# Moving weights, gate parts and X to other places in SBUF: a spectral layer with a gated FFN in float32r

## The chip, the cores and the metric

One core of one Trainium2 chip runs the whole program. The metric is the device time of one execution in microseconds; lower is better.

## The reference

For each of 8 sequences of 3008 rows and 256 channels, the reference takes a real FFT along the sequence, multiplies by a complex 256x256 weight, shrinks real and imaginary parts towards zero by 0.01, transforms back, and then runs a feed-forward layer over all 24064 rows:

```python
X = np.fft.rfft(x, axis=1)
Yr = Xr @ w_r - Xi @ w_i + b_r
Yi = Xr @ w_i + Xi @ w_r + b_i
Y* = sign(Y*) * max(abs(Y*) - 0.01, 0)
y = np.fft.irfft(Y, n=3008, axis=1)
h = y @ w_in                    # 256 -> 2048
g = h * clip(h + 3, 0, 6) / 6
out = g @ w_out                 # 2048 -> 256
```

The weights w_in and w_out come as float64, the output is float32.

## The kernel before

Each float32 operand is split into a high and a low part in float32r, and a product is three matmuls: low weight by high data, and high weight by high and by low data (`product`, line 137 is its matmul). The FFT is done as two small transforms (47 and 64 points) by matmuls, one sequence at a time: `stage1` (xs against f47), `middle` (bt against f64; then X against w_r, w_m and w_i, which stream while a block of X is the stationary operand; then z against g64) and `segment` (qt against f47, which writes `raw`, a tile of 512 output columns).

The FFN runs over 47 chunks c of 512 rows and, within each, over 8 bands f of 256 hidden columns: 376 units. In `prepare` the chunk's activations become seven blocks yb of 128x256, which are combined with seven 128x128 blocks of w_in per band (a Strassen-like scheme: `block`, in `phase_1`, `phase_2`, `phase_b` to `phase_e`): 21 matmuls of 256 columns. `gate` turns a unit's hidden values h into g, high and low part, in the tile `gs`: ScalarE's relu (line 1091), VectorE's multiply (line 1093), ScalarE's high part (line 1096), VectorE's low part (line 1097). `down` multiplies by w_out into two accumulators po0 and po1: 12 matmuls of 512 columns.

The order is written out by hand: the last loop goes unit by unit, with phases of unit i, of i - 1, the gate of i - 1 and i - 2, and four groups of `down` of i - 3, and between them `fill` puts one step of the FFT of the next sequence, by slots laid out in advance. So the engines' queues have a fixed order, and PE's is a mix of groups of three matmuls of each kind. The weights are made ready in the first hundred microseconds by the class `Band` (`upper`, `lower`, `sums_hi`, `sums_lo`), between the steps of the first sequence's FFT.

Tiles are laid out in SBUF in the order in which they are made, each at a multiple of 32 bytes in every partition: the constants first (weights among them), then the shared buffers by tag. The line `space([P, 24], F32, "gap")` makes a tile that nothing uses; what is made for the first time after it (X, z, the small buffers) lies 96 bytes further on. Each w_in band has 7 blocks of 512 bytes in a high and in a low tile, each w_out band 4 blocks of 512 bytes in each, so that all of them lie at the same place modulo 256.

Of the kernel before, what the change touches and what calls it, by code (L numbers as in the profile page):

```python
# [9 lines left out]
F32 = mybir.dt.float32  # L10
F32R = mybir.dt.float32r
# [3 lines left out]
ALU = mybir.AluOpType  # L15
# [6 lines left out]
B, S, D, FF = 8, 3008, 256, 2048  # L22
# [3 lines left out]
P = 128  # L26
# [4 lines left out]
NFT = FF // P  # L31

T = 512
# [68 lines left out]
def spectral_ffn(ctx: ExitStack, tc: tile.TileContext, x, w_r, w_i, bias, w_in, w_out, f47, f64, g64, g64u, sgn, out):  # L102
    nc = tc.nc
    const = ctx.enter_context(tc.tile_pool(name="const", bufs=1))
# [9 lines left out]
    def space(shape, dt, name, tag=None):  # L114
        tag = tag or name
        return sb.tile(shape, dt, name=name, tag=tag, bufs=depth.get(tag, 1))
# [11 lines left out]
    def split(hi, lo, src, on=None):  # L128

        nc.scalar.copy(out=hi, in_=src)  # L130
        (on or nc.vector).tensor_tensor(out=lo, in0=src, in1=hi.bitcast(F32), op=ALU.subtract)  # L131

    def product(ps, terms, start=True, stop=True, more=False, later=False):

        todo = [p for (ah, al), (bh, bl) in terms for p in (((al, bh), (ah, bh), (ah, bl)) if later else ((al, bh), (ah, bl), (ah, bh)))]
        for n, (a, b) in enumerate(todo):
            nc.tensor.matmul(  # L137
                out=ps,
                lhsT=a,
                rhs=b,  # L140
                start=start and n == 0,
                stop=stop and n == len(todo) - 1,
                skip_group_check=more,
            )
# [13 lines left out]
    nf = NFT // 2  # L158
# [8 lines left out]

    win_s = [const.tile([P, nf, 7, P], F32R, name="w_in_" + t) for t in ("hi", "lo")]  # L170
    wout_s = [const.tile([P, NFT * D], F32R, name="w_out_" + t) for t in ("hi", "lo")]
    under = const.tile([P, 1], F32, name="under")
    nc.vector.memset(under, -LAM)

# [27 lines left out]
    class Band:  # L202
# [56 lines left out]
        def upper(self):  # L259
            if self.into:  # L260
                nc.scalar.copy(out=win_s[0][:, self.f, :3], in_=self.value[:, 1:])
            else:
                nc.scalar.copy(out=wout_s[0][:, self.f * 512 : (self.f + 1) * 512], in_=self.top)

        def lower(self):
            f = self.f
            if not self.into:
                on = nc.gpsimd if f < nf - 2 else nc.vector
                on.tensor_tensor(
                    out=wout_s[1][:, f * 512 : (f + 1) * 512], in0=self.rf, in1=self.base, op=ALU.mult  # L270
                )

        def sums_hi(self):
# [18 lines left out]
    def band():  # L292

        n = len(bands)
        if n < len(todo_bands):
            bands.append(Band(*todo_bands[n], LATE.get(n) or SETS[n % len(SETS)]))
# [417 lines left out]
    next(mid)  # L714
    nc.sync.dma_start(out=sgn_s, in_=sgn)
    band()
    space([P, 24], F32, "gap")
    band()
    nc.sync.dma_start(out=g64u_s, in_=g64u)
    nc.sync.dma_start(out=bias_s[P // 2 :], in_=bias[P // 2 :])  # L720
# [12 lines left out]
    def part(pair, sl):  # L733
        return tuple(t[:, sl] for t in pair)
# [230 lines left out]
    def prepare(c):  # L965
        y = raw.pop(c) if c else raw[c]
        b11, b12, b21, b22 = y[:, 0, :H], y[:, 0, H:], y[:, 1, :H], y[:, 1, H:]
        s = space([P, 4, H], F32, "T")
        on = nc.gpsimd if c else nc.vector
        sums = [(0, b12, b11), (1, b22, s[:, 0]), (2, b22, b12), (3, b21, s[:, 1])]  # L970

        def sum_(n=1):
            for to, p, q in sums[:n]:
                on.tensor_tensor(out=s[:, to], in0=p, in1=q, op=ALU.subtract)
            del sums[:n]

        parts = [(2, b21), (1, b11), (6, s[:, 1]), (7, s[:, 2]), (5, s[:, 0]), (4, s[:, 3]), (3, b22)]
        if c:
            sum_(4)
        else:  # L980
            for n, src in parts[:2]:
                t = space([P, 2, H], F32R, "yb")
                yb[c, n] = (t[:, 0], t[:, 1])
                nc.scalar.copy(out=t[:, 0], in_=src)
                yield
            sum_(2)
            for n, src in parts[:2]:
                hi, lo = yb[c, n]
                on.tensor_tensor(out=lo, in0=src, in1=hi.bitcast(F32), op=ALU.subtract)
            del parts[:2]  # L990
        yield
        for n, src in parts:
            if c == 0:
                sum_({7: 1, 4: 1}.get(n, 0))
            t = space([P, 2, H], F32R, "yb")
            split(t[:, 0], t[:, 1], src, nc.gpsimd if n < 3 else on)
            yb[c, n] = (t[:, 0], t[:, 1])
            yield

    units = [(c, f) for c in range(NC) for f in range(nf)]  # L1000
    hs, ps_of, keep, gs, pos = {}, {}, {}, {}, {}
# [9 lines left out]
    def added(i, u, half, ps, n):  # L1011
        nc.vector.tensor_tensor(out=hs[i][:, u, half * H : (half + 1) * H], in0=ps, in1=keep.pop((i, n)), op=ALU.add)  # L1012
# [57 lines left out]
    def phase_e(i):  # L1070
        pc = keep.pop((i, "pc"))
        block(i, 3, pc, False)
        added(i, 0, 1, pc, "u2")

    def gate(i):

        h = hs.pop(i)
        if i == len(units) - 1:
            r = space([P, 2, T], F32, "r")
            t = gs[i] = space([P, 2, 2, T], F32R, "gs")  # L1080
            for u in (1, 0):
                nc.scalar.activation(out=r[:, u], in_=h[:, u], func=AF.Relu, bias=three, scale=1.0)
                nc.vector.scalar_tensor_tensor(
                    out=r[:, u], in0=r[:, u], scalar=6.0, in1=h[:, u], op0=ALU.min, op1=ALU.mult
                )
                split(t[:, 0, u], t[:, 1, u], r[:, u])
            yield
            return
        r = space([P, 2, T], F32, "r")
        for u in range(2):  # L1090
            nc.scalar.activation(out=r[:, u], in_=h[:, u], func=AF.Relu, bias=three, scale=1.0)  # L1091
        yield
        nc.vector.scalar_tensor_tensor(out=r, in0=r, scalar=6.0, in1=h, op0=ALU.min, op1=ALU.mult)  # L1093
        t = gs[i] = space([P, 2, 2, T], F32R, "gs")
        for u in range(2):
            nc.scalar.copy(out=t[:, 0, u], in_=r[:, u])  # L1096
        nc.vector.tensor_tensor(out=t[:, 1], in0=r, in1=t[:, 0].bitcast(F32), op=ALU.subtract)  # L1097
        yield

    def down(i, u, dh):  # L1100
        c, f = units[i]
        ft = 2 * f + u
        ends = i == len(units) - 1
        first, last = f == 0 and u == 0, f == nf - 1 and u == (0 if ends else 1)
        if first:
            pos[dh] = ps_o.tile([P, 512], F32, name=f"po{dh}")
        g = gs[i]
        product(
            pos[dh],
            later=True,  # L1110
            terms=[(part(wout_s, slice(ft * D + dh * P, ft * D + (dh + 1) * P)), (g[:, 0, u], g[:, 1, u]))],
            start=first,
            stop=last,
        )
        if last:
            ot = space([P, T], F32, "ot")
            if ends and dh:
                for n, at in enumerate((slice(0, H), slice(H, T))):
                    if n:
                        nc.vector.tensor_scalar(  # L1120
                            out=ot[:, at], in0=pos[dh][:, at], scalar1=1.0 / 6.0, scalar2=None, op0=ALU.mult
                        )
                    else:
                        nc.scalar.mul(out=ot[:, at], in_=pos[dh][:, at], mul=1.0 / 6.0)
                    nc.sync.dma_start(
                        out=out[dh * P : (dh + 1) * P, c * T + n * H : c * T + (n + 1) * H], in_=ot[:, at]
                    )
                return
            if dh:
                nc.vector.tensor_scalar(out=ot, in0=pos[dh], scalar1=1.0 / 6.0, scalar2=None, op0=ALU.mult)  # L1130
            else:
                nc.scalar.mul(out=ot, in_=pos[dh], mul=1.0 / 6.0)
            nc.sync.dma_start(out=out[dh * P : (dh + 1) * P, c * T : (c + 1) * T], in_=ot)
# [88 lines left out]
    for c in range(1, NC):  # L1222
        g = prepare(c)
# [5 lines left out]
    g = behind(later())  # L1229
    for q in (0, 6, 8, 9, 11, 13, 15, 17, 18, 19, 20, 22, 45):  # L1230
        slots.setdefault(q, []).append(g)
    g = stage1(1)
# [30 lines left out]
    n = len(units)  # L1263
# [8 lines left out]
    for i in range(n + 3):  # L1272
        if i > 1:
            part_of(phase_2, i)
        gated(i - 2)
        fill(4 * i)
        group(i - 3, 0)
        if i > 1:
            part_of(phase_1, i)
        part_of(phase_c, i - 1)  # L1280
        fill(4 * i + 1)
        group(i - 3, 1)
        fill(4 * i + 2)
        group(i - 3, 2)
        part_of(phase_b, i)
        part_of(phase_d, i - 1)
        fill(4 * i + 3)
        group(i - 3, 3)
        if 0 <= i - 3 < n:
            gs.pop(i - 3)  # L1290
        part_of(phase_e, i - 1)
        if 0 <= i - 1 < n:
            gates[i - 1] = gate(i - 1)
            gated(i - 1)
# [47 lines left out]
```

## Time and profile before

| | |
|---|---|
| median of three runs | 2561.31 us (2559.88 to 2561.36) |
| the profiled execution's own time | 2561.39 us |
| its span, first to last instruction | 2559.6 us |
| PE (matmuls) | 2541.4 us busy, 99%, 16510 matmuls |
| PEld (weight loads) | 2276.4 us busy, 89% |
| DVE, ACT | 1955.4 and 1955.5 us busy, 76% each |
| POOL | 734.7 us busy, 29% |
| granted TensorE clock | 1.000 on the mean |

A matmul's recorded duration includes the time in which it drains while the next one already runs, so durations of neighbours overlap; the busy time of a group counts overlapping time once. Two matmuls of one shape can be compared by their durations, and the distance between them is read from their starts in the timeline.

### The profile page before, as it was taken

The page shows a single profiled execution, that of the slowest core. Times are in us where ns is not written, and L with a number is a line of the kernel's source. Part 1 is how long each engine was busy: PE and PEld are TensorE (multiplying, and loading weights), DVE is VectorE, ACT ScalarE, POOL GpSimd, SP SyncE. Part 2 cuts the span into 40 slices and gives each one's busy share as a digit, 9 for nine tenths or more (in the row PEclk, how much of TensorE's full clock was granted, in tenths as well). Part 3 has the DMA queues.
Part 4 walks back from the last instruction along what each step waited for, and adds up shares of the span by engine and source line. Part 5 has one row for each costly group of instructions (what it writes and reads, how often), then busy time and mean ns, then how long its engine had stood idle before and what let it go on. Part 6 is the DMA issues. An engine that isn't in the chain of part 4 may idle for free.

```text
span 2559.6 us, 45563 instructions
## 1 busy us (share of the span) xinstructions
PE 2541.4 (99%) x16510; PEld 2276.4 (89%) x16510; DVE 1955.4 (76%) x3176; ACT 1955.5 (76%) x4329; POOL 734.7 (29%) x716
## 2 busy tenths in 40 slices
PE   9999999999999999999999999999999999999999
PEld 6788889899999989988899888998999999999998
DVE  6988877777777877777777777777777777777676
ACT  5777777777777777777777777777777777777877
POOL 3223422333133421433313432134311221121210
PEclk9999999999999999999999999999999999999999
DMA  8534422232122221232212332222321121110000
GB/s 282 171 97 137 128 74 72 83 93 76 54 83 80 90 80 51 82 84 81 82 55 77 92 87 67 65 77 82 90 60 59 56 69 53 37 32 25 20 17 17
DMA packets 147321, 199.75 MB, mean 78 GB/s; under 512 B 16319, under 2 KB 102039, under 8 KB 147095
## 3 DMA queue, kind: packets, MB, share of 16 engines
q1 hardware_dynamic: 147095, 196.83, 25.7%
q8 instruction: 130, 2.13, 0.4%
q14 instruction: 96, 0.79, 0.1%
HBM read 99.77 MB, written 74.97 MB: 68 GB/s over the span
## 4 chain that ended last, share of the span: by engine, by line
PE 88%; DVE 4%; ACT 4%; issue 2%; DMA 1%; POOL 1%; SPq 0%; DVEq 0%; ACTq 0%; POOLq 0%
PE po L137 37%; PE ps_a L137 24%; PE pb L137 18%; PE ps_a L869 3%; PE ps_a L755 2%; PE ps_a L471 1%; DVE r L1093 1%; ACT gs L1096 1%; DVE gs L1097 1%; ACT r L1091 1%; DMA xin<-in_x 1%; DVE h L1012 1%; PE ps_a L506 0%; PE pb L438 0%; DVE tc L794 0%
## 5 line engine op out<-in xcount | busy, mean ns | idle before, releaser
L137 PE MATMUL po<-gs,w_out_hi 128*128 128x512 f32 x3008 | 947.5, 395 | 1.1 <-DVE gs L1097 0.9
L1091 ACT ACTIVATE r<-h,three 128x512 f32<-128x512 f32 x750 | 541.1, 725 | 148.5 <-DVE h L1012 133.1
L1093 DVE SCALAR_TENSOR_TENSOR r<-r,h 128x1024 f32<-128x1024 f32 x375 | 489.6, 1306 | 209.5 <-ACT r L1091 208.6
L137 PEld LDWEIGHTS po<-gs,w_out_hi 128*128 128x128 f32 x3008 | 566.3, 189 | 85.1 <-DVE gs L1097 5.1
L137 PE MATMUL po<-gs,w_out_lo 128*128 128x512 f32 x1504 | 610.0, 406 | 0.2 <-ACT gs L1096 0.2
L1097 DVE TENSOR_TENSOR gs<-r,gs 128x1024 fp32r<-128x1024 f32 x375 | 479.2, 1278 | 162.0 <-ACT gs L1096 161.6
L1096 ACT CAST gs<-r 128x512 fp32r<-128x512 f32 x750 | 429.2, 620 | 180.3 <-DVE r L1093 173.1
L137 PE MATMUL pb<-yb,w_in_hi 128*128 128x256 f32 x3004 | 554.8, 278 | 0.0
L137 PEld LDWEIGHTS pb<-yb,w_in_hi 128*128 128x128 f32 x3004 | 458.4, 188 | 33.8
L131 POOL TENSOR_TENSOR yb<-T,yb 128x256 fp32r<-128x256 f32 x184 | 194.7, 1060 | 841.7 <-ACT yb L130 841.3
L137 PE MATMUL ps_a<-yb,w_in_hi 128*128 128x256 f32 x2252 | 428.6, 279 | 0.0
L137 PE MATMUL pb<-yb,w_in_lo 128*128 128x256 f32 x1502 | 421.8, 281 | 3.1 <-ACT u L1009 1.7
L1012 DVE TENSOR_TENSOR h<-ps_a,u 128x256 f32<-128x256 f32 x752 | 313.6, 417 | 120.4 <-PE ps_a L137 117.6
L137 PEld LDWEIGHTS ps_a<-yb,w_in_hi 128*128 128x128 f32 x2252 | 344.1, 188 | 16.0 <-DVE yb L131 0.2
L1009 ACT COPY u<-pb 128x256 f32<-128x256 f32 x752 | 279.1, 372 | 97.0 <-PE pb L137 95.8
L137 PE MATMUL ps_a<-yb,w_in_lo 128*128 128x256 f32 x1126 | 316.7, 281 | 4.6 <-DVE h L1012 4.3
L137 PEld LDWEIGHTS pb<-yb,w_in_lo 128*128 128x128 f32 x1502 | 282.0, 188 | 40.0 <-ACT u L1009 3.4
L137 PEld LDWEIGHTS po<-gs,w_out_lo 128*128 128x128 f32 x1504 | 283.4, 188 | 20.5 <-issue 2.3
L137 PEld LDWEIGHTS ps_a<-yb,w_in_lo 128*128 128x128 f32 x1126 | 211.5, 188 | 28.3 <-DVE h L1012 11.4
L1009 ACT COPY p<-pb 128x256 f32<-128x256 f32 x376 | 138.4, 368 | 33.3 <-PE pb L137 30.8
L1012 DVE TENSOR_TENSOR h<-ps_a,p 128x256 f32<-128x256 f32 x376 | 156.3, 416 | 2.1 <-ACT p L1009 1.4
L131 POOL TENSOR_TENSOR xs<-xin,xs 120x512 fp32r<-120x512 f32 (+1 forms) x42 | 55.2, 1313 | 308.5 <-ACT xs L130 299.6
(189 smaller groups left out, 3454.9 us busy)
## 6 DMA issues: line engine op xcount, KB each, us to landing
xin<-in_x SPq DMA_DIRECT2D x48, 512.0 KB, 3.7
bt<-scr SPq DMA_DIRECT2D x96, 256.0 KB, 3.2
scr<-pt SPq DMA_DIRECT2D x96, 256.0 KB, 2.0
out<-ot SPq DMA_DIRECT2D x93, 256.0 KB, 2.0
scr<-a SPq DMA_DIRECT2D x96, 240.0 KB, 2.5
qt<-scr SPq DMA_DIRECT2D x96, 240.0 KB, 3.5
zt<-tc SPq DMA_DIRECT2D x336, 64.0 KB, 2.0
f<-in_f SPq DMA_DIRECT2D x96, 128.0 KB, 2.9
```

What stands on the lines that cost most here:

```text
L131: (on or nc.vector).tensor_tensor(out=lo, in0=src, in1=hi.bitcast(F32), op=ALU.subtract)
L137: nc.tensor.matmul(out=ps, lhsT=a, rhs=b, start=start and n == 0, stop=stop and n == len(todo) - 1, skip_group_check=more,)
L471: nc.tensor.matmul(out=to, lhsT=x[:, xh, dh, which], rhs=w_s[w][wh][:, dh * D : (dh + 1) * D], start=False, stop=n == 2 and (which, dh) == ...
L755: nc.tensor.matmul(out=psv[:, dh, :, u, :], lhsT=data[:, u, dh * P : (dh + 1) * P], rhs=f[:, u, :], start=True, stop=True,)
L869: nc.tensor.matmul(out=ps[:, cs * w + g * rows : cs * w + (g + 1) * rows], lhsT=qt[:rows, cs, g, dh * P : (dh + 1) * P], rhs=f47_s[2][:row ...
L1009: nc.scalar.copy(out=t, in_=ps)
L1012: nc.vector.tensor_tensor(out=hs[i][:, u, half * H : (half + 1) * H], in0=ps, in1=keep.pop((i, n)), op=ALU.add)
L1091: nc.scalar.activation(out=r[:, u], in_=h[:, u], func=AF.Relu, bias=three, scale=1.0)
L1093: nc.vector.scalar_tensor_tensor(out=r, in0=r, scalar=6.0, in1=h, op0=ALU.min, op1=ALU.mult)
L1096: nc.scalar.copy(out=t[:, 0, u], in_=r[:, u])
L1097: nc.vector.tensor_tensor(out=t[:, 1], in0=r, in1=t[:, 0].bitcast(F32), op=ALU.subtract)
```

## The change

The high and low parts of w_in become one tile with, per band, seven high blocks, seven low ones and 8 bytes that nothing uses; w_out likewise, with four and four. So the bands step by 8 bytes more than a multiple of 256. A second unused tile of 128 bytes is made after them. The gate's tile gets 256 bytes more, and its 4 x 512 values start in it at a place that depends on the chunk (`PLACES`, in bytes). The unused tile ahead of X shrinks from 96 to 64 bytes. No instruction is added or taken away, and no order is changed.

```diff
-    win_s = [const.tile([P, nf, 7, P], F32R, name="w_in_" + t) for t in ("hi", "lo")]
-    wout_s = [const.tile([P, NFT * D], F32R, name="w_out_" + t) for t in ("hi", "lo")]
+    win = const.tile([P, nf, 14 * P + 2], F32R, name="w_in")
+    win_s = [win[:, :, n * 7 * P : (n + 1) * 7 * P].rearrange("p f (n c) -> p f n c", n=7) for n in range(2)]
+    BAND = 4 * D + 2
+    wout = const.tile([P, nf * BAND], F32R, name="w_out")
+    wout_s = [wout[:, : nf * BAND - 2 * D], wout[:, 2 * D :]]
+    const.tile([P, 32], F32, name="gap")
...
-                nc.scalar.copy(out=wout_s[0][:, self.f * 512 : (self.f + 1) * 512], in_=self.top)
+                nc.scalar.copy(out=wout_s[0][:, self.f * BAND : self.f * BAND + 512], in_=self.top)
...
-                    out=wout_s[1][:, f * 512 : (f + 1) * 512], in0=self.rf, in1=self.base, op=ALU.mult
+                    out=wout_s[1][:, f * BAND : f * BAND + 512], in0=self.rf, in1=self.base, op=ALU.mult
...
-    space([P, 24], F32, "gap")
+    space([P, 16], F32, "gap")
...
+    PLACES = (0, 64, 128, 192, 32, 96, 16, 80, 8, 72, 48, 112, 4, 68, 24, 160)
+
+    def gate_parts(i):
+
+        at = PLACES[units[i][0] % len(PLACES)] // 4
+        t = space([P, 4 * T + 64], F32R, "gs")[:, at : at + 4 * T]
+        return t.rearrange("p (n u c) -> p n u c", n=2, u=2)
+
...
-            t = gs[i] = space([P, 2, 2, T], F32R, "gs")
+            t = gs[i] = gate_parts(i)
...
+        at = f * BAND + u * D + dh * P
...
-            terms=[(part(wout_s, slice(ft * D + dh * P, ft * D + (dh + 1) * P)), (g[:, 0, u], g[:, 1, u]))],
+            terms=[(part(wout_s, slice(at, at + P)), (g[:, 0, u], g[:, 1, u]))],
```

## Rows read from the trace of the kernel before

**Rows 1.** The page: busy time by engine, the chain by engine.
```profile
PE 2541.4 (99%) x16510; PEld 2276.4 (89%) x16510; DVE 1955.4 (76%) x3176; ACT 1955.5 (76%) x4329; POOL 734.7 (29%) x716
...
PE 88%; DVE 4%; ACT 4%; issue 2%; DMA 1%; POOL 1%; SPq 0%; DVEq 0%; ACTq 0%; POOLq 0%
```

**Rows 2.** Busy time of each engine in stretches, with the granted clock.
```profile
0.00:100.00 100.00, 96.18 (x574) 69.84 (x575) 74.86 (x139) 64.75 (x133) 29.42 (x42) 1.00 0.77 254
...
1000.00:1500.00 500.00, 498.03 (x3262) 450.83 (x3261) 387.39 (x630) 386.06 (x859) 162.39 (x146) 1.00 0.27 79
```

**Rows 3.** Matmul groups, costliest first: busy us, mean ns; idle before, releaser.
```profile
L137 PE MATMUL po<-gs,w_out_hi 128*128 128x512 f32 x3008 | 947.5, 395 | 1.1 <-DVE gs L1097 0.9
L137 PE MATMUL po<-gs,w_out_lo 128*128 128x512 f32 x1504 | 610.0, 406 | 0.2 <-ACT gs L1096 0.2
L137 PE MATMUL pb<-yb,w_in_hi 128*128 128x256 f32 x3004 | 554.8, 278 | 0.0
L137 PE MATMUL ps_a<-yb,w_in_hi 128*128 128x256 f32 x2252 | 428.6, 279 | 0.0
L137 PE MATMUL pb<-yb,w_in_lo 128*128 128x256 f32 x1502 | 421.8, 281 | 3.1 <-ACT u L1009 1.7 <-ACT p L1009 1.3
L137 PE MATMUL ps_a<-yb,w_in_lo 128*128 128x256 f32 x1126 | 316.7, 281 | 4.6 <-DVE h L1012 4.3
```

**Rows 4.** The same view: w_m_hi is as w_r_hi; w_i_lo, w_m_lo as w_i_hi.
```profile
L137 PE MATMUL ps_a<-w_r_hi,X 128*128 128x256 f32 x336 | 73.8, 282 | 0.3 <-DVE X L131 0.3
...
L137 PE MATMUL ps_a<-w_i_hi,X 128*128 128x256 f32 x336 | 73.5, 281 | 0.0
L137 PE MATMUL ps_a<-z,g_hi 128*128 128x512 f32 x168 | 52.5, 393 | 0.0
L137 PE MATMUL ps_a<-w_r_lo,X 128*128 128x256 f32 x168 | 47.4, 282 | 0.0
...
L137 PE MATMUL ps_a<-z,g_lo 128*128 128x512 f32 x84 | 33.3, 397 | 0.7 <-DVE h L1012 0.7
...
L471 PE MATMUL ps_a<-w,X 128*128 128x256 f32 x144 | 23.3, 283 | 0.0
```

**Rows 5.** By tile: duration in ns, shortest/median/longest, first and last start.
```profile
L137 PE MATMUL pb<-yb,w_in_hi x3004: 276/276/286, 104.6 to 2549.1; 128*128 128x256 f32 x188
...
L137 PE MATMUL po<-gs,w_out_hi x3008: 388/394/506, 112.9 to 2555.7; 128*128 128x512 f32 x188
...
L137 PE MATMUL ps_a<-w_r_hi,X x336: 276/282/392, 187.1 to 2197.9; 128*128 128x256 f32 x168
...
L471 PE MATMUL ps_a<-w,X x144: 274/283/283, 28.3 to 88.4; 128*128 128x256 f32 x144
```

**Rows 6.** Timeline of PE: start us, us, engine, line, op, tiles, count.
```profile
407.18 0.63 PE L137 MATMUL po<-gs,w_out_hi 128*128 128x512 f32 x2
407.64 0.28 PE L137 MATMUL pb<-yb,w_in_lo 128*128 128x256 f32 x1
...
408.67 0.39 PE L137 MATMUL po<-gs,w_out_lo 128*128 128x512 f32 x1
```

**Rows 7.** Timeline of PE: the first of eighteen on X, and what follows the last.
```profile
770.16 0.28 PE L137 MATMUL ps_a<-w_r_hi,X 128*128 128x256 f32 x1
...
772.32 0.39 PE L137 MATMUL po<-gs,w_out_lo 128*128 128x512 f32 x1
```

**Rows 8.** Timelines of PE, then of the weight loads, around 1251 us.
```profile
1251.02 0.28 PE L137 MATMUL pb<-yb,w_in_lo 128*128 128x256 f32 x1
...
1252.08 0.28 PE L137 MATMUL ps_a<-w_r_hi,X 128*128 128x256 f32 x1
...
1251.02 0.31 PEld L137 LDWEIGHTS pb<-yb,w_in_hi 128*128 128x128 f32 x2
```

**Rows 9.** By tile: VectorE's write of gs (duration shortest/median/longest).
```profile
L1097 DVE TENSOR_TENSOR gs<-r,gs x375: 1207/1226/2351, 113.0 to 2549.9; 128x1024 fp32r<-128x1024 f32 x188
```

More of the change, by code (lines that the diff above doesn't have):

```diff
@@ L1093, in gate @@
         nc.vector.scalar_tensor_tensor(out=r, in0=r, scalar=6.0, in1=h, op0=ALU.min, op1=ALU.mult)
-        t = gs[i] = space([P, 2, 2, T], F32R, "gs")
+        t = gs[i] = gate_parts(i)
         for u in range(2):
```

## The prediction

> **What bounds the kernel now.** I read the page's busy shares and chain first, then the table of stretches, the groups of matmuls by line and shape, the durations of one tile's instructions, and last a few microseconds of the timeline.
>
> TensorE is busy for 2541.4 of 2559.6 us, and 88% of the chain that ended last is its work [rows 1]. The stretches say the same: 498.03 of 500 us in the middle and 96.18 of the first 100 us, at a granted clock of 1.00, the level of 2.4 GHz [rows 2]. So there is hardly a wait to win or lose. What can move the time is the pace of the matmuls themselves, and 7884 of 256 columns (activations yb against w_in) and 4512 of 512 columns (gs against w_out) are most of them [rows 3].
>
> The reader is to see that this pace isn't one number. A matmul's recorded duration holds a part that overlaps the next, so I compare durations of one shape and take spacing from starts in the timeline. The shape 128x256 stands at 278 to 281 ns with yb [rows 3], but at 281 to 282 ns with X and at 283 ns in the first batch's X (line 471) [rows 4], and single ones go from 276 to 283 [rows 5]. In spacing: nine matmuls on yb go from 407.64 to 408.67, 114 ns each [rows 6]; the eighteen on X from 770.16 to 772.32, 120 ns each [rows 7]; elsewhere nine on yb go from 1251.02 to 1252.08, 118 ns each [rows 8]. Nothing is waited for in any of them. The weight load of the next matmul starts with each matmul (1251.02 and 1251.02) [rows 8], so two streams are read from SBUF side by side, and which bytes they are on at one moment follows from where the tiles lie and from the moment at which they started. That yb runs at 114 and at 118 with the same places says that the start matters; that X never comes down to yb's 276 as its usual value (its median is 282, against 276 for line 137's yb into pb) [rows 5] lets the places matter too.
>
> The places follow from the order and sizes of the tiles in the code. Modulo 256 bytes: every w_in and w_out block starts at 192, every yb and gs part at 128, w_r, w_i, w_m at 128, X at 224. So the place of the streamed operand less that of the stationary one is 192 for yb and gs, 160 for X, and 0 for the first batch's X, which lies in gs's buffer. z against g64 has 96. Durations grow in the order 192 (279), 160 (282), 0 (283) for 256 columns [rows 3, 4].
>
> **The change, part by part.**
> *w_in bands step by 8 bytes.* A band is 7168 bytes of high and low plus 8, so band f starts at 192 + 8f and the difference for yb becomes 192 - 8f: 192, 184, ..., 136. No instruction is added. The weighted mean now is (278x3004 + 279x2252 + 281x1502 + 281x1126)/7884 = 279.3 ns; X's, at 160, is (282x672 + 281x336 + 282x168 + 281x336)/1512 = 281.6 ns [rows 3, 4]. Band 4 gets exactly X's difference. I price bands 4 to 7 at X's 2.3 ns more, bands 1 to 3 at a quarter, a half and three quarters of it: (1.5 + 4)/8 x 2.3 x 7884 = **+12.5 us**. The bounds: bands 1 to 7 all at the slowest row, 283, cost 3.7 x 7884 x 7/8 = +25.5; all at the shortest, 276 [rows 5], give 3.3 x 7884 x 7/8 = -22.8.
> *w_out bands and the gate's parts.* w_out now starts at 0 + 8f and gs at 128 plus 0 to 192 by chunk, so the difference takes nearly every multiple of 8 (and two of 4) instead of 192. The nearest row of 512 columns is z (difference 96): (393x168 + 397x84)/252 = 394.3 ns, against 395 for gs on w_out_hi [rows 3, 4]. It argues for nothing; twice X's 2.3 ns, as it is twice the columns, argues for +4.6. I take +1.5, nearer to the row of the same width: 1.5 x 4512 x 15/16 (an estimate that one chunk place in sixteen is like now) = **+6.3 us**. Bounds: +4.6 gives +19.5; gs's own shortest, 388 against 395 [rows 5], gives -29.6.
> *X at 192.* 96 bytes of gap become 64, gs grows by 512 in all, and the constants by 256 (64 + 64 for the bands, 128 for the new gap): X moves from 224 to 192, its difference from 160 to 192, yb's present one. At yb's duration, 2.3 x 1512 = **-3.5 us**. Bounds: 0, and 281.6 - 276 = 5.6 x 1512 = -8.5. The first batch's X stays at 0. z goes from 96 to 64; 252 matmuls at a few ns are under 1.5 us either way: 0.
> *What is costed at nothing.* ScalarE and VectorE write gs at new places (VectorE's write takes 1226 ns at the median) [rows 9]; they are busy 76% [rows 1], and the matmuls on gs waited 1.1 and 0.2 us in all [rows 3]; if the writes grew by a fifth they would still fit. High and low in one tile could add a wait where the bands are prepared; TensorE then idles 3.8 of the first 100 us [rows 2], and I allow for as much again: 0 to +3.8.
>
> Sum: 12.5 + 6.3 - 3.5 = +15.3 us on the profiled execution's 2561.4, which is the median (2561.31) to 0.1: **2577 us**, +0.6%. A measurement tells about 0.2%, 5 us, from no change.
>
> **A rule that speaks for no effect.** The 118 and 120 ns in [rows 7, 8] come without any wait, with weight loads beside them. The Trainium skill, "SBUF — State Buffer", section "Who interferes with whom", gives TensorE two read ports, one for the moving operand and one for LDWEIGHTS, independent, and says that it never waits for anyone. By that the sum would be 0; by the rows it is +15.3. The trace agrees only in that no engine's work stands between these matmuls; it doesn't show why one shape has several paces.
>
> **The rivals.**
> *Slower, as above* (0.45): 2577, its own range 2564 to 2600. For: of the known differences yb's 192 is the quickest for 256 columns, and most matmuls leave it. Against: yb alone holds 114 and 118, so the start may matter more than the place.
> *Places don't matter* (0.17): the pace is set by the moment at which a group starts, and X's 120 by what runs before it. Then X's -3.5 and the rest cancel or are absent: 2558 to 2566, no change. For: z's rows of 512 columns at another difference equal gs's. Against: 283 is nearly every duration of line 471 (its median and its longest) [rows 5].
> *The slow pattern breaks up* (0.27), the case on the other side: at 192 a group that starts badly stays at 118 to its end [rows 8]; with a difference that changes by band and chunk, the streams slide against each other and fall into the 114 pattern. All of it would be -22.8 - 29.6 - 8.5 = -61; half is -30: 2531. It decides once more than about a quarter of the moved matmuls come down to their shortest, since that outweighs the +15.3. For: 276 is the median already in one group of yb. Against: neither X nor line 471, at other differences, has that median.
> *Starts off a 16-byte line* (0.11): odd bands start at 8 modulo 16, so a block of 512 bytes lies on 33 lines of 16 bytes instead of 32. A load that takes a thirty-second longer of the 114 ns in which loads follow each other [rows 6] costs 3.6 x 7884 / 2 = +14, and streams of gs in the five of sixteen chunk places that aren't multiples of 16 a 128th of 231 ns (from 407.18 to 407.64 for two [rows 6]), 1.8 x 4512 x 5/16 = +2.5: 2594. The Trainium skill, same page, "Specifications (TRN2)", says that SBUF has lines of 16 bytes and that each crossing to a new line pays; no matmul of this trace has an operand that starts off 16, so none shows it.
>
> **How the numbers follow.** Slower by over 0.2%: 0.45 + 0.11, less a little of the first that ends near zero, 0.55; no change 0.18; faster 0.27. The range leaves out the better half of the faster case and the tail of the line case with the upper bounds: 2535 to 2608. The likeliest case alone has 2564 to 2600.
>
> **What would show each step.** If it is right, yb's matmuls in pb and ps_a rise from 279 towards 281 or 282 with waits unchanged, X's fall to 279 or so, gs's rise by 1 to 2 ns, and the bands differ: f = 0 keeps its pace, f = 4 to 7 run like X now. Busy shares, clock and waits stay. The prediction is wrong if yb's mean falls towards 276, if X stays at 282 in spite of its new difference, if gs moves by more than 5 ns, or if the first 100 us grow.

## The result, and the profile after

The changed kernel takes 2575.72 us (three runs, 2574.64 to 2576.27) against 2561.31: 1.0057 of the time before, with a 95% interval of 1.0035 to 1.0080. It is slower by some 14 us; 2577 was forecast.

The page of the kernel after, its busy times and its chain by engine, against [rows 1]:

```profile
PE 2555.2 (99%) x16510; PEld 2288.6 (89%) x16510; DVE 1954.5 (76%) x3176; ACT 1964.2 (76%) x4329; POOL 729.7 (28%) x716
...
PE 91%; DVE 3%; ACT 3%; issue 1%; DMA 1%; POOL 0%; SPq 0%; DVEq 0%; ACTq 0%; POOLq 0%
```

The count of matmuls is the same to the last one, and TensorE's busy time grew by 13.8 us while the span grew by 13.3 (2559.6 to 2572.9). So no wait came in: the matmuls themselves follow each other more slowly. The view of groups by line and shape says which (w_in and w_out now are one tile each, so high and low stand in one row), against [rows 3, 4]:

```profile
L137 PE MATMUL po<-gs,w_out 128*128 128x512 f32 x4512 | 1281.6, 400 | 1.4 <-DVE gs L1109 0.8 <-ACT gs L1108 0.2
L137 PE MATMUL pb<-yb,w_in 128*128 128x256 f32 x4506 | 659.1, 281 | 3.0 <-ACT u L1013 1.6 <-ACT p L1013 1.4
L137 PE MATMUL ps_a<-yb,w_in 128*128 128x256 f32 x3378 | 525.6, 281 | 3.7 <-DVE h L1016 3.0
...
L137 PE MATMUL ps_a<-w_r_hi,X 128*128 128x256 f32 x336 | 72.2, 279 | 0.3 <-DVE X L131 0.3
L137 PE MATMUL ps_a<-w_i_hi,X 128*128 128x256 f32 x336 | 71.7, 278 | 0.0
...
L137 PE MATMUL ps_a<-w_r_lo,X 128*128 128x256 f32 x168 | 46.8, 279 | 0.0
...
L475 PE MATMUL ps_a<-w,X 128*128 128x256 f32 x144 | 23.3, 283 | 0.0
```

yb's mean went from 279.3 to 281 ns, X's from 281.6 to 278 or 279, and gs's, over high and low, from (395x3008 + 406x1504)/4512 = 398.7 to 400; the first batch's X, whose difference of places stayed at 0, stands at 283 as before. The third number after the bar, idle time, is as small as it was.

The durations by tile (shortest/median/longest, against [rows 5]) show that the shortest hardly moved (276 to 274 for yb) and the usual one did: yb's median in pb, 276 for the high part and 281 for the low one before, is 281 over both, and X's went from 282 to 276, 277 or 278.

```profile
L137 PE MATMUL pb<-yb,w_in x4506: 274/281/389, 105.1 to 2562.4; 128*128 128x256 f32 x196
...
L137 PE MATMUL ps_a<-w_r_hi,X x336: 276/277/388, 188.2 to 2206.1; 128*128 128x256 f32 x168
L137 PE MATMUL ps_a<-w_m_hi,X x336: 276/276/358, 188.9 to 2206.8; 128*128 128x256 f32 x168
...
L475 PE MATMUL ps_a<-w,X x144: 280/283/283, 29.3 to 88.9; 128*128 128x256 f32 x144
```

In the timeline after, nine matmuls on yb take from 195.42 to 196.49, 119 ns each; eighteen on X take from 220.51 to 222.56, 114 ns each, where before they took 120 [rows 7]:

```profile
195.42 0.87 PE L137 MATMUL pb<-yb,w_in 128*128 128x256 f32 x6
196.13 0.52 PE L137 MATMUL ps_a<-yb,w_in 128*128 128x256 f32 x3
196.49 0.63 PE L137 MATMUL po<-gs,w_out 128*128 128x512 f32 x2
...
220.51 0.28 PE L137 MATMUL ps_a<-w_r_hi,X 128*128 128x256 f32 x1
...
222.56 0.64 PE L137 MATMUL po<-gs,w_out 128*128 128x512 f32 x2
```

For a finer account I take the distance from each matmul's start to the next one's, over all of the trace, and set distances that hold a wait apart (over 130 ns for 256 columns, over 260 for 512). Summed with the waits, yb's 7896 distances went from 930.0 to 946.6 us (+16.6), gs's 4511 from 1076.0 to 1078.2 (+2.2), X's 1512 from 180.3 to 174.6 (-5.7): +13.1 of the span's 13.3. Without the waits the means are 115.9 to 118.2 ns for yb, 232.0 to 232.9 for gs, and 118.9 to 115.2 for X. "Pace" below is this mean.

### The profile page after: what moved, and what is told of

Same layout as the page of the kernel before. It is cut to its first block, busy times and chain, and to the rows that moved or that the text cites. A ratio compares the mean times of both kernels' runs of the same rounds, so it can differ in the third digit from the quotient of the medians.

```text
span 2572.9 us, 45563 instructions
## 1 busy us (share of the span) xinstructions
PE 2555.2 (99%) x16510; PEld 2288.6 (89%) x16510; DVE 1954.5 (76%) x3176; ACT 1964.2 (76%) x4329; POOL 729.7 (28%) x716
## 4 chain that ended last, share of the span: by engine, by line
PE 91%; DVE 3%; ACT 3%; issue 1%; DMA 1%; POOL 0%; SPq 0%; DVEq 0%; ACTq 0%; POOLq 0%
PE po L137 38%; PE ps_a L137 25%; PE pb L137 19%; PE ps_a L873 3%; PE ps_a L759 3%; PE ps_a L475 1%; DVE gs L1109 1%; ACT gs L1108 1%; ACT r L1103 1%; DVE h L1016 1%; DVE r L1105 0%; PE ps_a L510 0%; DMA xin<-in_x 0%; PE pb L442 0%; DMA qt<-scr 0%
## 5 line engine op out<-in xcount | busy, mean ns | idle before, releaser
L137 PE MATMUL po<-gs,w_out 128*128 128x512 f32 x4512 | 1281.6, 400 | 1.4 <-DVE gs L1109 0.8
L137 PEld LDWEIGHTS po<-gs,w_out 128*128 128x128 f32 x4512 | 770.1, 189 | 109.8 <-issue 4.2
L137 PEld LDWEIGHTS pb<-yb,w_in 128*128 128x128 f32 x4506 | 638.9, 188 | 72.9 <-ACT p L1013 3.3
L137 PE MATMUL pb<-yb,w_in 128*128 128x256 f32 x4506 | 659.1, 281 | 3.0 <-ACT u L1013 1.6
L137 PE MATMUL ps_a<-yb,w_in 128*128 128x256 f32 x3378 | 525.6, 281 | 3.7 <-DVE h L1016 3.0
L137 PEld LDWEIGHTS ps_a<-yb,w_in 128*128 128x128 f32 x3378 | 478.6, 188 | 42.5 <-DVE h L1016 9.6
L1072 ACT COPY h<-pb 128x256 f32<-128x256 f32 x376 | 141.6, 377 | 2.9 <-PE pb L137 2.8
L131 POOL TENSOR_TENSOR yb<-raw,yb 128x256 fp32r<-128x256 f32 x138 | 128.9, 943 | 44.9 <-ACT yb L130 44.8
L873 PEld LDWEIGHTS ps_a<-f_all,qt 120*128 120x128 f32 x816 | 107.8, 191 | 11.4 <-PE pb L405 1.7
L873 PE MATMUL ps_a<-f_all,qt 120*128 120x120 f32 x816 | 108.1, 273 | 1.2 <-DMA qt<-scr 1.2
```

The source lines that it names most:

```text
L137: nc.tensor.matmul(out=ps, lhsT=a, rhs=b, start=start and n == 0, stop=stop and n == len(todo) - 1, skip_group_check=more,)
L873: nc.tensor.matmul(out=ps[:, cs * w + g * rows : cs * w + (g + 1) * rows], lhsT=qt[:rows, cs, g, dh * P : (dh + 1) * P], rhs=f47_s[2][:row ...
L1072: nc.scalar.copy(out=hs[i][:, 1, :H], in_=pb)
```

## The experiments

Three theories. **Theory 1**: the difference of places modulo 256, streamed operand less stationary block, sets a matmul's pace. **Theory 2**: the value doesn't matter, but groups that follow each other with unlike differences cost. **Theory 3**: places don't matter. Each of the twelve kernels was timed against the kernel before on the same chip (2562.4 to 2562.6 us there). In each, filler tiles keep all that isn't named at its old place modulo 256. But for the kernels that move gs, the operands streamed against w_in, w_out and X start at 128 modulo 256, so "a difference of 184" could as well be read as "a block that starts at 200"; no run moved yb, and the two readings aren't told apart.

| kernel | time, us | ratio to before, 95% interval | pace of yb, X, gs, ns |
|---|---|---|---|
| before | 2562.4 to 2562.6 | 1 | 115.9, 118.9, 232.0 |
| X alone at 192 | 2556.35 | 0.9975 (0.9966 to 0.9985) | 115.8, 115.2, 232.1 |
| w_in bands step by 8 bytes, alone | 2577.73 | 1.0059 (1.0046 to 1.0071) | 118.1, 118.5, 232.6 |
| w_out bands and gate places alone | 2569.10 | 1.0029 (1.0019 to 1.0039) | 116.6, 119.0, 232.7 |
| all of w_in at 160 | 2570.17 | 1.0030 (1.0019 to 1.0041) | 117.2, 117.5, 232.4 |
| w_in in one tile, places as before | 2562.51 | 0.9999 (0.9990 to 1.0009) | 116.0, 118.8, 232.0 |
| all of w_in at 184 | 2578.73 | 1.0061 (1.0049 to 1.0074) | 118.4, 118.0, 232.5 |
| w_in bands at 192 and 160 in turn | 2575.04 | 1.0047 (1.0035 to 1.0060) | 117.8, 118.4, 232.4 |
| w_in bands step by 32 bytes | 2579.41 | 1.0063 (1.0051 to 1.0076) | 118.2, 118.1, 232.9 |
| all of w_in at 64 | 2574.62 | 1.0047 (1.0035 to 1.0060) | 117.8, 117.7, 232.2 |
| all of w_in at 0 | 2578.45 | 1.0063 (1.0049 to 1.0077) | 117.9, 118.1, 233.3 |
| X at 192, all of w_out at 248 | 2553.99 | 0.9963 (0.9950 to 0.9975) | 115.8, 113.9, 231.3 |
| X at 192, first batch's X too | 2557.52 | 0.9980 (0.9971 to 0.9989) | 115.8, 115.3, 232.1 |

### The three parts of the change, each alone

X alone:

```diff
-    space([P, 24], F32, "gap")
+    space([P, 16], F32, "gap")
```

> Only X moves, from a difference of 160 to 192 bytes; weights and gate parts stay as before. Theory 1 (the difference of places sets the pace): X's 1512 matmuls fall from 282 to about 278 ns as they did in the changed kernel, 5 to 6 us less, some 2555.5 us, ratio 0.998. Theory 2 (what costs is that neighbouring groups have unlike differences): X now has the same difference as yb and gs around it, so it gains as well, and the time is the same 2555.5. Theory 3 (places don't matter): 2561, X stays at 282 ns.

6.3 us less. The groups by line of this kernel show X at 278 and 279 ns, yb at 277 and 279 (278 and 279 before [rows 3]):

```profile
L137 PE MATMUL pb<-yb,w_in_hi 128*128 128x256 f32 x3004 | 553.5, 277 | 0.0
L137 PE MATMUL ps_a<-yb,w_in_hi 128*128 128x256 f32 x2252 | 429.0, 279 | 0.0
...
L137 PE MATMUL ps_a<-w_r_hi,X 128*128 128x256 f32 x336 | 72.0, 279 | 0.4 <-DVE X L131 0.3
...
L137 PE MATMUL ps_a<-w_i_hi,X 128*128 128x256 f32 x336 | 71.7, 278 | 0.0
```

A tile that nothing uses, made 32 bytes smaller, moves the time beyond its interval: theory 3 falls here.

The bands of w_in alone (high and low in one tile as in the change, and 192 bytes of filler behind it):

```diff
-    win_s = [const.tile([P, nf, 7, P], F32R, name="w_in_" + t) for t in ("hi", "lo")]
+    win = const.tile([P, nf, 14 * P + 2], F32R, name="w_in")
+    win_s = [win[:, :, n * 7 * P : (n + 1) * 7 * P].rearrange("p f (n c) -> p f n c", n=7) for n in range(2)]
+    const.tile([P, 48], F32, name="gap_b")
```

> Only the bands of w_in step by 8 bytes; all else lies as before modulo 256. Theories 1 and 2: yb's 7896 matmuls take about 2.1 ns more each, as in the changed kernel, +16 us, about 2577 us. Theory 3: 2561 us.

15.1 us more, nearly all of it in yb's distances (930.0 to 945.2 us; gs's grew by 2.5, X's fell by 1.0). By band, from difference 192 down to 136, the pace is 116.1, 118.1, 118.7, 117.2, 117.9, 118.5, 119.2 and 119.1 ns. The one band that stayed at 192 keeps its pace, against theory 2; the next, 8 bytes away, has already lost 2 ns.

w_out's bands and the gate's places alone (the change's own lines, with w_in and the gap ahead of X as before):

> Only w_out's bands and the gate's parts move; w_in and X lie as before modulo 256. From the changed kernel's trace gs's matmuls take 0.9 ns more: +3 to +4 us, 2564 to 2565 us by theory 1. By theory 2 yb's groups, which follow gs's groups, start worse too: yb rises from 279 ns by about 1 ns, +8 us on top, 2572. Theory 3: 2561.

6.5 us more. gs's distances grew by 2.7 us (1076.0 to 1078.7) and yb's by 5.2 (930.0 to 935.2), although neither yb nor w_in had moved; the median of yb's high part in pb went from 276 [rows 5] to 280, that in ps_a stayed at 280:

```profile
L137 PE MATMUL pb<-yb,w_in_hi x3004: 276/280/290, 106.0 to 2558.8; 128*128 128x256 f32 x188
L137 PE MATMUL ps_a<-yb,w_in_hi x2252: 276/280/383, 106.9 to 2559.9; 128*128 128x256 f32 x188
```

So the neighbours of a group matter as well as its own places, as theory 2 has it. The distances sorted by their place in a run of yb show where. The last matmul on yb before one on gs went from 115.2 to 118.0 ns (829 of them, 2.3 us); beside it the next block, one of w_out, is loaded, as weight loads start with the matmul before theirs [rows 8], and w_out had moved. After a group on gs, the first four distances on yb went from 119.1, 115.8, 115.3 and 115.1 ns to 117.9, 117.6, 116.7 and 115.8; from the fifth on both kernels stand between 115.0 and 115.5. What the group before leaves wears off here within four matmuls.

gs's own rise has another cause, which the distances sorted by chunk show. In the eleven of sixteen chunk places that are multiples of 16 bytes gs's pace is 231.9 ns, where the same chunks had 232.0 before, although their differences to w_out range over the multiples of 8. At 8, 24 and 72 it is 233.6 and at 4 and 68 it is 235.9, where those chunks had 232.0 before. The whole change repeats it: 232.0, 233.8 and 236.3. So it is streams that start off a multiple of 16 bytes that cost on gs, 3.4 us in all, and on the mean not the difference. The view by tile has it for a chunk at place 112 and the next one, at place 4:

```profile
L137 PE MATMUL po<-gs,w_out x94: 388/394/482, 736.6 to 788.9; 128*128 128x512 f32 x94
L137 PE MATMUL po<-gs,w_out x94: 390/398/483, 790.7 to 842.9; 128*128 128x512 f32 x94
```

The three parts add up: 15.1 + 6.5 - 6.3 = 15.3 us, against 14.4 for the change.

### Value or unlike neighbours

One common place for all of w_in, 32 bytes on (filler of 8 values ahead, 56 behind):

```diff
+    const.tile([P, 8], F32, name="gap_a")
     win_s = [const.tile([P, nf, 7, P], F32R, name="w_in_" + t) for t in ("hi", "lo")]
+    const.tile([P, 56], F32, name="gap_b")
```

> All of w_in moves by 32 bytes, so that every yb product has the one difference 160 (band 4's in the changed kernel, X's before). Theory 1: yb's pace is band 4's, 118.4 ns, or X's before, 118.9, against 115.9: +19 to +23 us, 2580 to 2584 us. Theory 2 (unlike differences of neighbours cost, not the value): within a run of yb all differences are alike again and only the passage from and to gs differs, so most of the cost goes: 2561 to 2567 us. Theory 3: 2561.

7.6 us more, between the two. As a control, and to try other places, w_in was made one tile with a table of places, in values, one for each band:

```diff
-    win_s = [const.tile([P, nf, 7, P], F32R, name="w_in_" + t) for t in ("hi", "lo")]
+    places = (0, 0, 0, 0, 0, 0, 0, 0)
+    win = const.tile([P, nf * 14 * P + 0], F32R, name="w_in")
...
+            at = [(14 * f + 7 * n) * P + p for f, p in enumerate(places)]
```

> Control: high and low parts of w_in in one tile, but every block still at its old place modulo 256 (difference 192 throughout). Theories 1 and 2: same as before, 2561 to 2563 us, yb at 279 ns. If the one tile itself (its waits, its layout) made the 8-byte steps slow, the time is near 2577 us.

No difference: one tile costs nothing. The filler behind it also moved all later tiles by 256 bytes against w_in, so a shift by 256 costs nothing either. With all places 2, all of w_in moves by 8 bytes:

> All of w_in moves by 8 bytes: one difference of 184 for every yb product. Theory 1 (the value sets the pace): band 1's pace of the changed kernel, 118.4 ns against 115.9, +19 us, 2581 us. Theory 2 (what costs is that neighbours are unlike): no more than the move by 32 bytes cost, 0 to +8 us, 2562 to 2570 us. If starts off a 16-byte line cost on their own, more than the 7.5 us of the move by 32 bytes.

16.4 us more, and nine matmuls on yb, from 232.23 to 233.31, at 120 ns, though here all of w_in has one difference:

```profile
232.23 0.88 PE L137 MATMUL pb<-yb,w_in 128*128 128x256 f32 x6
232.95 0.52 PE L137 MATMUL ps_a<-yb,w_in 128*128 128x256 f32 x3
233.31 0.28 PE L137 MATMUL ps_a<-w_r_hi,X 128*128 128x256 f32 x1
```

Theory 2 alone falls: within yb nothing is unlike, and the time is that of the stepped bands. Nor is it the passage from gs: at the fifth to eighth matmul on yb behind it the pace is still 118.4 to 118.9 ns. With places 0 and 8 in turn (each odd band's last eight low weights then share their place with the next band's first eight high ones, so these weights are changed):

> Even bands of w_in at a difference of 192 as before, odd ones at 160. Theory 1: the mean of the two kernels that have one of them throughout, +4 us, 2566 us. Theory 2: neighbours are always unlike, so more than either, +10 to +15 us, 2573 to 2578 us.

12.7 us more, where the mean of the two uniform kernels is 3.8: bands at 192 now stand at 117.5 ns and those at 160 at 118.2, against 115.9 and 117.2 when each is alone. So unlike neighbours cost too, but not at the passage itself: a distance between matmuls of unlike bands is 117.4 ns on the mean, one between matmuls of the same band 118.0 (116.1 before). With places 0, 8, 16 to 56:

> Bands of w_in step by 32 bytes instead of 8, so the differences are 192, 160, 128, 96, 64, 32, 0 and 224. Theory 2: as slow as the 8-byte steps, +13 to +18 us, about 2577 us, every band at 117.5 ns or more, the one at 192 too. Theory 1: the bands spread from 115.9 (192) to 120 (0), as the first batch's X stood at; the middle, 118, gives the same +16, but then the band at 192 stands at 116.

17.1 us more. By difference, from 0 up to 224 by 32: 118.8, 117.8, 117.9, 119.1, 118.7, 117.5, 117.5 and 118.4 ns. Steps of 32 bytes are as slow as steps of 8, and 192 among the others has lost its lead, as theory 2 expected. In the steps of 8 it had kept it (116.1), so how much a neighbour costs depends on its place as well.

### Other common places, and a faster kernel

Filler of 32 values ahead of w_in and 32 behind, then 48 and 16:

> All of w_in at a difference of 64 instead of 192. If the place counts modulo 128, the pace of yb is as before, 115.9 ns, and the time 2562. If it counts modulo 256, yb goes to about 118 ns, as the other places tried, +16 us, 2578. By places not mattering at all (already at odds with the earlier runs): 2562 and every passage as before.

12.2 us more: 64 isn't 192, so the place doesn't count modulo 128 only.

> All of w_in at a difference of 0, where the first batch's X stands at 119.9 ns with hardly a spread. If the difference's value sets the pace, yb goes to 119 to 120 ns from 115.9: +24 to +32 us, 2586 to 2594 us. If only unlike neighbours cost, no more than the move to 160 cost, 2562 to 2570.

16.1 us more, yb at 117.9 and not at 119 to 120: a difference has no pace of its own that it carries from one pair of tiles to another, since the first batch's X has the same 0 and 119.8.

X at 192 with all of w_out at one new place (200 bytes on, in one tile):

```diff
+    const.tile([P, 48], F32, name="gap_a")
+    wout = const.tile([P, 2 * NFT * D + 8], F32R, name="w_out")
+    wout_s = [wout[:, 2 + n * NFT * D : 2 + (n + 1) * NFT * D] for n in range(2)]
+    const.tile([P, 8], F32, name="gap_b")
```

> X at 192 as in the run that moved it alone (2556), and all of w_out at a difference of 248 from gs, which had the lowest mean of the places in the changed kernel (230.6 ns over 42 intervals, against 232.0 before). If that value holds for a uniform place: 1.4 ns on 4272 intervals, 6 us less, 2550 us. If a difference other than 192 between gs and yb disturbs the passage between their groups: yb's pace rises and the time is 2556 to 2566.

2554 us, 8.4 below before: faster than both kernels. Against X alone (0.9975) the intervals overlap, so a gain from w_out's new place isn't shown in the time. gs's pace fell by 0.7 ns, half of what 42 distances in the changed kernel promised, and X's to 113.9. yb's mean stayed, but not its make-up: behind a group on gs its distances now run 117.6, 118.9, 116.3 and then 113.9 to 114.1, where with X alone they ran 118.8, 115.5, 115.3 and then 114.7 to 115.4. yb and w_in lie as in that kernel, so even the pace at which a run settles moved with w_out's place.

```profile
L137 PE MATMUL po<-gs,w_out 128*128 128x512 f32 x4512 | 1274.9, 398 | 1.8 <-DVE gs L1100 0.9 <-ACT ot L1135 0.6 <-ACT gs L1099 0.2
L137 PE MATMUL pb<-yb,w_in_hi 128*128 128x256 f32 x3004 | 555.9, 278 | 0.0
```

X at 192 in the first batch too:

```diff
-                xt[g // 2] = space([P, 2, 2, 2, 2, P], F32R, "X", "gs")
+                t = space([P, 16 * P + 64], F32R, "X", "gs")[:, 16 : 16 + 16 * P]
+                xt[g // 2] = t.rearrange("p (a b h r c) -> p a b h r c", a=2, b=2, h=2, r=2)
```

> X of the later batches at 192 (2556) and the first batch's X, which lies in gs's buffer, at 192 instead of 0 as well: its 288 matmuls fall from 119.9 to about 115 ns, 1.4 us less if they are on the path there, so 2555; 2556 if the first stage waits for other work anyway.

The first batch's X does come down, its pace from 119.8 to 115.8 ns, but that is 1.2 us, and the time can't be told from X's later batches alone (0.9980 and 0.9975, with overlapping intervals).

```profile
L472 PE MATMUL ps_a<-w,X x144: 276/281/282, 28.8 to 87.7; 128*128 128x256 f32 x144
```

## Why the prediction was right, by its steps

**What bounds it.** TensorE's own pace, without waits: it held. All of the change is in distances between matmuls that wait for nothing.

**w_in's bands, +12.5 us.** Right in sign, and in that leaving 192 costs; 15.1 when done alone. X's loss as the price for band 4 came out in the changed kernel (118.3 ns, X 118.9 before), but all of w_in at X's 160 stood at 117.2, so the price doesn't belong to the difference alone. What failed is the gradual price: bands 1 to 3 were to pay a quarter, a half and three quarters of X's loss, but the band 8 bytes off paid 2.2 ns at once and the kernel with all of w_in 8 bytes off is the dearer one (1.0061 against 1.0030 for 32 bytes). Nothing falls off with distance; 192 was one good place, and every other one tried for w_in was worse. "f = 0 keeps its pace" held when only w_in moved (116.1 ns) and not in the whole change (117.3), where its neighbours on gs and w_out had moved as well.

**w_out and the gate, +6.3 us.** 6.5 when done alone, but in that trace gs's matmuls, which were to pay all of it, grew by 2.7 and yb's by 5.2. And gs didn't pay for differences that leave 192: at places that are multiples of 16 its pace stayed (231.9 against 232.0). The term was right by two causes that it left out, what runs before and beside a group, and streams off a multiple of 16, which the prediction had only among its rivals. That it came out to 0.2 us is luck.

**X, -3.5 us.** -6.3, of which 5.6 lie in X's distances (180.3 to 174.7 us): the way was right, the size too small. The term took durations, in which X stood 2.3 ns above yb; in distances it was 3.0. And it took yb's mean as X's new pace, which holds the slow first matmuls behind gs (119.1 ns); from the third on yb stands at 115.1 to 115.5, and X, which runs as eighteen matmuls of one kind and mostly behind yb, came to 115.2.

**What was costed at nothing.** One tile for high and low: 0.9999. The first matmul of line 137 on yb into pb starts at 105.1 us instead of 104.4, and between 104.3 and 105.8 in the other runs that leave the first batch as it was, so that is scatter.

**The sum.** +15.3 forecast, +14.4 measured. w_in's term was 2.6 us too small and X's gain 2.8 too small; that these two cancel is luck too.

**The rival that places don't matter** fell with X alone, and with it the sum of 0 that the prediction drew from a rule: the Trainium skill, "SBUF — State Buffer", section "Who interferes with whom", has TensorE's two read ports independent and TensorE waiting for no one. Here no instruction waits in the profile, but 32 bytes of an unused tile are worth 6.3 us, and 8 bytes under w_in 16.4; where a sum of 0 and the measurement differ, the measurement decides. Whether the two ports, or another engine's accesses, are at work in it isn't shown.

**The rival that the slow pattern breaks up** fell: no kernel with mixed places had yb below 116.6 ns.

**The rival of 16-byte lines** (its terms add up to 2593, not 2594) came out for streams and not for weight loads. gs's five places off a multiple of 16 were to cost 1.8 ns a matmul, 2.5 us; they cost 1.6 ns at 8, 24 and 72 and 3.9 at 4 and 68, 3.4 us, the whole of gs's rise. Why 4 costs more than 8 stays open. Blocks of weights that start off 16 show no such cost: the stepped bands of w_in off a multiple of 16 (184, 168, 152, 136) have a mean of 118.2 ns, those on one but 192 (176, 160, 144) 118.6, and among the chunks at multiples of 16 w_out's odd bands, which start off 16, have 231.8 ns and the even ones 231.9. The uniform move of w_in by 8 bytes was dearer than those by 32, 128 and 192 bytes (16.4 against 7.6, 12.2 and 16.1 us), by next to nothing against the last; a small cost of such loads is neither shown nor excluded.

Theory 1 and theory 2 each hold in part: the value counts (five common places of w_in give 0, 7.6, 12.2, 16.1 and 16.4 us), and so does what the group before leaves. Why 192 suits yb, and what inside the memory or the engine makes places cost, stays open: the profile shows starts, not accesses.

## What to carry to other kernels

When TensorE is busy all the time and matmuls of one shape have several durations with no wait between them, the places of their operands in SBUF are worth a trial: move one tile by some tens of bytes with filler and compare the group's mean and median. Look for one common place that suits a whole run of matmuls and keep it for its neighbours; a mixture took the slow value here, and a good place for one pair of tiles couldn't be carried to another by its number. Start a streamed operand at a multiple of 16 bytes: off it a matmul of 512 columns took 1.6 to 3.9 ns more. A total that comes out right can hide terms that were wrong in place: only the parts done alone, and their distances sorted by chunk and by place in a run, showed that yb paid for the gate's move and gs for the starts of its streams.

## What the runs showed of the hardware

The 256-column matmul with a weight load for each came at 113 to 114 ns at best (9 on yb [rows 6], 18 on X in the timeline above) and 118 to 120 at worst, at full granted clock in both. Between kernels only places changed; but within the kernel before nine on yb take 114 and 118 at the same places [rows 6, 8], so a place sets how often a pace comes and not each one. Moving w_in also moved X's pace, at X's own unchanged place, from 118.9 to 117.5 ns (w_in at 160), and moving w_out moved X's from 115.2 to 113.9: what a group leaves reaches into the next, for four matmuls on yb when w_out and gs moved by band and chunk, through all eighteen on X when w_out moved as one (113.6 to 113.8 at every place of a run behind yb). A stream of 512 columns that started 8 bytes off a multiple of 16 took 1.6 ns more, at 4 bytes (places 4 and 68) 3.9 ns more; weight blocks that started at 8 modulo 16 show no cost of their own.
